# FFN gate weights loaded as 112 partitions on all DMA engines and twice 8 partitions on the lower eight engines

**Chip and metric.** One core of a Trainium2 chip (trn2). The metric is device time in microseconds, the median of several runs; "rounds" are runs of two kernels taken in turn on the same chip. Some executions are slower; only fast runs are compared.

## The reference

One decode step of eight sequences: layer norm, 32 query heads on 8 key/value heads over the last 1,024 positions, output projection, times the silu of a gated FFN. Nearly all of the time is reading 47 MB once (the data queue's packets fill 95.3% of the span on 16 engines): K and V (34 MB), and the weights.

```python
def _A_ref(x, k_cache, v_cache, wq, wo):
    W = min(4096, max(256, Sk // 4))                 # 1024
    q = (x @ wq).reshape(B, Sq, Hq, Dh).transpose(0, 2, 1, 3)
    k = jnp.repeat(k_cache[:, :, Sk - W:, :], rep, axis=1)
    ...
    p = _softmax(scores, axis=-1)
    ...
def _B_ref(x, w_gate, w_up, w_down):
    return (_gelu(x @ w_gate) * (x @ w_up)) @ w_down   # 512 -> 1792 -> 512

xn = _layernorm(x)
return x + _A_ref(xn, ...) * _silu(_B_ref(xn, ...))
```

## The kernel before

All large loads are issued by SyncE on one queue, in the order in which they are needed; the program runs ahead, with eight transfers in flight (the trace has eight completion semaphores, used in turn). The FFN weights come last but for the output weights `wo`.

```python
def load_wide(rows, c0, c1):
    t = wide_slot()                                   # [128, 8192] bf16, one of three buffers
    nc.sync.dma_start(out=t[:, 0 : c1 - c0], in_=rows[:, c0:c1])
    return t

def load_up(w):                                       # 128 rows of 7168 bf16 = 14,336 bytes
    return load_wide(w.rearrange("(p k) n -> p (k n)", k=NDC), 0, NDC * F)
# ... cut ...
for g in range(NGR + 1):                              # NGR = 16 groups of K and V
    if g < NGR:
        v_t[g] = load_kv(A_v_cache, *groups[g])       # 128 rows of 8,192 bytes each
        if g + 2 < NGR:
            k_t[g + 2] = load_kv(A_k_cache, *groups[g + 2])
    if g == NGR - 1:
        wg_t = load_up(B_w_gate)
        wu_t = load_up(B_w_up)
        wd_t = load_down()
    if g == NGR:
        parts = [(0, 16), (16, 24), (24, 28), (28, 30), (30, 31), (31, 32)]
        wo_t = [load_wo(*q) for q in parts[:2]]       # the first takes the gate's buffer
        # ... cut ...
```

The softmax here doesn't subtract the row's maximum and nothing guards it: scores larger than these inputs give would overflow.

## Time and profile before

| | before |
|---|---|
| time, median (range) | 120.83 us (120.68 to 120.94) |
| span of the profiled run | 118.8 us |
| DMA, mean of 16 engines in mid-run | busy all the time, 427 GB/s |
| TensorE, VectorE, ScalarE busy | 73%, 52%, 34% |
| last weight piece lands, engine by engine | 113.90 to 115.50 us |

The lines are in the prediction. The DMA engines never rest (share 1.00 to 1.01 from 20 to 113.5 us), so only their slowest decides. Each transfer is split over engines, and the trace holds one packet record per row and one completion per engine (16 for the gate load of 128 rows, 8 for each of the two loads of `x_sb`, which have 8 rows), without the engine's name. As packets of one engine follow each other without a gap (each starts 3 ns before the recorded end of the last), they can be chained into 16 lanes by their times alone; "lane" below means that. Where packets are lengthened, that overlap scatters up to some 25 ns and two lanes can be swapped, so there a lane is the likeliest chain, and what counts is read from packets and completions without lanes.

Nearly all rows take the same time: of the 4,224 rows of 8,192 bytes on the data queue all but 14 took 309 ns, seven of the 14 longer by 9 ns at most; of the 384 rows of 14,336 bytes all but one took 535 or 540 ns. A "fetch" below is a packet on the queue that the page calls instruction; there are seven in the span, of 16,384 bytes, and the prediction lists when they came and what they cost.

### The profile page before, as it was taken

How to read it: one execution, taken by the hardware profiler on the slowest of the kernel's cores; microseconds unless marked ns; L12 is line 12 of the kernel's file. 1: busy time of each engine (PE TensorE's matmuls, PEld its weight loads, DVE VectorE, ACT ScalarE, POOL GpSimd, SP SyncE). 2: the span in 40 equal slices, each digit the busy share in tenths (PEclk: the TensorE clock that was granted, in tenths of full speed). 3: DMA queues.
4: the chain of work that ended last, by engine and by line, in shares of the span. 5: the costliest groups of instructions: out<-in, count | busy, mean ns of one | idle time of the engine just before them, and what ended most of it. 6: DMA issues, size and time to landing. Idle time of an engine off the chain costs nothing.

```text
span 118.8 us, 2378 instructions
## 1 busy us (share of the span) xinstructions
PE 86.6 (73%) x985; PEld 59.4 (50%) x985; DVE 62.0 (52%) x131; ACT 40.5 (34%) x78; POOL 4.8 (4%) x14
## 2 busy tenths in 40 slices
PE   0005946786989899799799798778959661898680
PEld 0004713653657567577477386456638340334670
DVE  5025645543756856956866764846728336420111
ACT  5000324792442552462462462442524303002000
POOL 5900000000000000000000000000000000000000
PEclk9999999555899999999999999999999996579999
DMA  4999999999999999999999999999999999999950
GB/s 88 437 394 436 419 433 425 422 433 419 428 428 430 422 417 436 417 430 428 419 422 436 425 417 433 428 425 425 422 428 446 419 449 415 440 438 400 409 193 3
DMA packets 6345, 47.61 MB, mean 401 GB/s; under 512 B 816, under 2 KB 1088, under 8 KB 1344
## 3 DMA queue, kind: packets, MB, share of 16 engines
q1 hardware_dynamic: 6304, 47.47, 95.3%
q8 instruction: 7, 0.11, 0.3%
q14 instruction: 2, 0.02, 0.0%
q10 hardware_dynamic: 32, 0.01, 0.0%
HBM read 47.46 MB, written 0.01 MB: 400 GB/s over the span
## 4 chain that ended last, share of the span: by engine, by line
DMA 58%; PE 24%; DVE 7%; ACT 4%; SPq 2%; issue 1%; DVEq 0%
DMA wide_slot<-in_B_w_gate_dram 18%; DMA slot<-in_A_v_cache_dram 16%; DMA slot<-in_A_wo_dram 12%; DMA wide_slot<-in_A_wq_dram 11%; PE t_ps L257 11%; DVE kT L263 4%; PE sc_ps L283 4%; PE o_ps L317 3%; ACT q_all L429 2%; PE a_ps L344 2%; DVE q_all L429 2%; PE big L567 1%; ACT L296 1%; PE sc_ps L273 1%; PE big L445 1%
## 5 line engine op out<-in xcount | busy, mean ns | idle before, releaser
L263 DVE COPY kT<-t_ps 128x1024 bf16<-128x1024 bf16 x48 | 31.7, 688 | 23.3 <-PE t_ps L257 21.4
L257 PE MATMUL t_ps<-ident_f,slot 128*128 128x128 f32 x256 | 38.3, 300 | 2.4 <-DMA slot<-in_A_k_cache_dram 2.2
L257 PEld LDWEIGHTS t_ps<-ident_f,slot 128*128 128x128 f32 x256 | 31.1, 153 | 12.5 <-issue 7.6
L263 ACT COPY kT<-t_ps 128x1024 bf16<-128x1024 bf16 x16 | 16.2, 1012 | 11.6 <-ACT p L296 5.0
L296 ACT ACTIVATE p<-sc_ps 128x512 bf16<-128x512 f32 x16 | 9.6, 597 | 30.1 <-PE sc_ps L283 30.0
L283 PE MATMUL sc_ps<-kT,q_all 128*32 128x512 bf16 x128 | 10.7, 406 | 7.6 <-DVE kT L263 5.8
L304 DVE STREAM_TRANSPOSE pT<-p 128x512 bf16<-128x512 bf16 x16 | 11.2, 703 | 2.7 <-ACT p L296 2.7
L317 PE MATMUL o_ps<-slot,pT 128*32 128x256 bf16 x256 | 9.9, 275 | 1.1 <-DVE pT L304 1.1
L344 PE MATMUL a_ps<-selr,o_sb 128*128 128x16 f32 x64 | 8.4, 263 | 0.0
L283 PEld LDWEIGHTS <-q_all 128*32 128x32 bf16 x128 | 2.0, 95 | 12.4 <-DVE kT L263 8.4
L344 PEld LDWEIGHTS a_ps<-selr,o_sb 128*128 128x128 f32 x64 | 7.8, 192 | 0.0
L225 PE MATMUL t_ps<-ident,xhat 32*128 32x32 bf16 x4 | 0.3, 194 | 10.3 <-DVE xhat L215 10.3
L317 PEld LDWEIGHTS <-pT 128*32 128x32 bf16 x256 | 5.4, 95 | 4.2 <-issue 2.5
L327 ACT COPY o_sb<-o_ps 128x256 f32<-128x256 f32 x16 | 6.0, 377 | 1.3 <-PE o_ps L317 1.3
L273 PE MATMUL sc_ps<-far,hot 4*128 4x512 bf16 x16 | 6.4, 398 | 0.0
L445 PE MATMUL big<-wide_slot,xT 128*32 128x448 bf16 x32 | 2.6, 463 | 4.3 <-DMA wide_slot<-in_B_w_up_dram 3.1
L225 PEld LDWEIGHTS <-xhat 32*128 32x128 bf16 x4 | 0.2, 114 | 10.2 <-DVE xhat L215 10.2
L567 PEld LDWEIGHTS <-og 128*32 128x32 bf16 x128 | 4.1, 97 | 2.2 <-issue 1.1
L366 PE MATMUL t_ps<-q_sb,ident 128*32 128x512 bf16 x14 | 4.8, 497 | 0.0
L353 DVE RECIPROCAL rs<-a_ps 128x32 f32<-128x32 f32 x8 | 2.9, 358 | 3.0 <-PE a_ps L344 3.0
L429 DVE COPY q_all<-t_ps 64x128 bf16<-64x128 bf16 x4 | 2.7, 778 | 2.4 <-ACT q_all L429 1.6
L429 ACT COPY q_all<-t_ps 64x128 bf16<-64x128 bf16 x4 | 2.7, 726 | 2.5 <-DVE q_all L429 2.5
(70 smaller groups left out, 54.2 us busy)
## 6 DMA issues: line engine op xcount, KB each, us to landing
slot<-in_A_k_cache_dram SPq DMA_DIRECT2D x16, 1024.0 KB, 19.6
slot<-in_A_v_cache_dram SPq DMA_DIRECT2D x16, 1024.0 KB, 19.6
wide_slot<-in_A_wq_dram SPq DMA_DIRECT2D x2, 2048.0 KB, 10.6
wide_slot<-in_A_wo_dram SPq DMA_DIRECT2D x1, 2048.0 KB, 12.3
wide_slot<-in_B_w_gate_dram SPq DMA_DIRECT2D x1, 1792.0 KB, 21.4
wide_slot<-in_B_w_up_dram SPq DMA_DIRECT2D x1, 1792.0 KB, 23.2
wide_slot<-in_B_w_down_dram SPq DMA_DIRECT2D x1, 1792.0 KB, 25.0
slot<-in_A_wo_dram SPq DMA_DIRECT2D x1, 1024.0 KB, 14.4
```

Of the source, the lines that this page charges most:

```text
L257: nc.tensor.transpose(kp[:, c * P : (c + 1) * P], kw[:, rp * P : (rp + 1) * P], ident_f)
L263: copy(out=kT_t[g][:, t * 8 * P : (t + 1) * 8 * P], in_=kp.bitcast(BF16))
L273: nc.tensor.matmul(sc, hot.rearrange("n r q -> n (r q)"), far, start=True, stop=False, skip_group_check=True,)
L283: nc.tensor.matmul(sc[32 * t : 32 * t + 32, :], q2_all[:, i, b, e, :, :, :].rearrange("w r n j -> w (r n j)"), kT[:, :, 32 * t : 32 * t + ...
L296: nc.scalar.activation(out=p, in_=sc_t[g], func=ACT.Exp, scale=inv_sqrt_dh, accum_out=acc)
L304: nc.vector.transpose(out=pT, in_=p)
L317: nc.tensor.matmul(o_ps[32 * u : 32 * u + 32, :], pT_t[g][:, m * 32 : (m + 1) * 32], v_t[g][:, m * 256 : (m + 1) * 256], start=(m < 4), st ...
L327: nc.scalar.copy(out=o_sb, in_=o_ps)
L344: nc.tensor.matmul(a_ps[:, 1, m, :], o_t[g + m][:, r * Dh : (r + 1) * Dh], selr[:, r, :], start=(r == 0), stop=(r == 1), skip_group_check= ...
L366: nc.tensor.matmul(idle[0:32, :], ident[:, 0:32], moving[:, 0:512], start=True, stop=True, skip_group_check=True,)
L429: copy(out=q2_all[64 * rr : 64 * rr + 64, i, :, e, rr, :, :].rearrange("p b n j -> p j n b"), in_=qT_ps[64 * rr : 64 * rr + 64, :, e, :, 0 ...
L567: nc.tensor.matmul(acc[a], shifted(og, j, q), wo_t[piece][:, c0 : c0 + DQ], start=(j == rows[0] and q == 0), stop=(j == rows[-1] and q == ...
```

## The change

The seven engines that finish 1.4 us early are to take work from those that finish late. Each of the two loads of `x_sb`, with 8 rows, made 8 packets and 8 completions: it ran on eight engines, here called the lower eight. So 16 of the gate's 128 rows are cut off and sent as two 8-row loads, while 112 rows go to all engines. If the pieces go to the same eight engines as `x_sb` and the 112 rows are dealt out evenly, 7 each, a lower engine has 9 rows and another 7; that was the plan, and the trace names no engine to check it by.

```diff
-    def load_wide(rows, c0, c1):
+    WHOLE, LOWER = [(0, P)], [(0, P - 16), (P - 16, P - 8), (P - 8, P)]
+
+    def load_wide(rows, c0, c1, pieces=WHOLE):
         t = wide_slot()
-        nc.sync.dma_start(out=t[:, 0 : c1 - c0], in_=rows[:, c0:c1])
+        for p0, p1 in pieces:
+            nc.sync.dma_start(out=t[p0:p1, 0 : c1 - c0], in_=rows[p0:p1, c0:c1])
         return t
-    def load_up(w):
-        return load_wide(w.rearrange("(p k) n -> p (k n)", k=NDC), 0, NDC * F)
+    def load_up(w, pieces=WHOLE):
+        return load_wide(w.rearrange("(p k) n -> p (k n)", k=NDC), 0, NDC * F, pieces)
@@
-            wg_t = load_up(B_w_gate)
+            wg_t = load_up(B_w_gate, LOWER)
```

## The prediction

> **What bounds the kernel now.** I read the page's slices first, then its DMA queues, then the chain that ended last, then the waits of the DMA-issuing queue.
>
> The slices and the queue lines:
>
> ```profile
> DMA  4999999999999999999999999999999999999950
> GB/s 88 437 394 436 419 433 425 422 433 419 428 428 430 422 417 436 417 430 428 419 422 436 425 417 433 428 425 425 422 428 446 419 449 415 440 438 400 409 193 3
> q1 hardware_dynamic: 6304, 47.47, 95.3%
> q8 instruction: 7, 0.11, 0.3%
> q14 instruction: 2, 0.02, 0.0%
> ```
>
> The 16 DMA engines are busy from the second slice to the third from the end, at some 427 GB/s, 26.7 GB/s each. TensorE at 73% and VectorE at 52% follow. So the kernel ends when the slowest DMA engine has moved its bytes. The chain of waits, cut to its last pieces, says the same:
>
> ```profile
> 75.69 21.41 DMA wide_slot<-in_B_w_gate_dram
> 97.15 0.94 PE big L445 x16
> ...
> 99.92 14.42 DMA slot<-in_A_wo_dram
> 114.33 0.04 issue
> 114.37 1.56 PE big L567 x32
> 115.96 0.29 DVE tmp L581
> 116.27 0.28 DVE out_sb L582
> ```
>
> After the last weight pieces only 3 us are left. The gate load stands on the chain because line 97 (the large output weight load) takes the gate's buffer, but that issue at 98.13 us comes some 6 us before the engines finish the down weights (103.9 to 105.6), so it starves nothing.
>
> The page gives the mean of the engines; the view by windows shows that they do not finish together:
>
> ```profile
> 110.00:113.50 3.50, 2.48 (x84) 2.36 (x85) 0.49 (x2) 0.00 (x0) 0.00 (x0) 1.00 1.00 401
> 113.50:114.20 0.70, 0.55 (x20) 0.42 (x15) 0.00 (x0) 0.00 (x0) 0.00 (x0) 1.00 0.66 241
> 114.20:115.60 1.40, 1.23 (x30) 1.23 (x30) 0.55 (x2) 0.00 (x0) 0.00 (x0) 1.00 0.32 113
> ```
>
> The DMA share (last column but one) falls from 1.00 to 0.66 to 0.32 before the end. The trace's completion events (one per engine and transfer) say how: of the last weight piece, seven engines complete at 113.90 to 114.13 us, one at 114.59, eight at 115.04 to 115.50. That 1.4 us is what the change is after: hand work from late engines to early ones.
>
> **Who is late, and why.** Ahead of 26 us all 16 engines complete each 1 MB within 0.36 us. Then single engines fall back by about 1.41 us, each just after a 16 KB packet of queue 8 (at 27.2, 42.0, 54.1, 67.0, 81.8, 92.5 and 112.3 us; 0.88 to 0.96 us of transfer, and the row queued beside it takes 0.76 to 1.03 us instead of 0.31 or 0.54); the two packets of queue 14 cost two others 0.5 to 0.85 us. Every other engine advances by exactly 2,453 ns per 1 MB, so the engines can be followed by phase. The two loads of x have 8 rows and put a 512-byte packet on eight engines: those are the "lower eight". Followed to the down weights (108.5 us), lateness in ns is: lower 0, 152, 158, 231, 762, 1199, 1440, 1551; the other eight 94, 169, 215, 225, 1509, 1584, 1606, 1675. The packet at 112.3 makes the 94 late too. So fetches hit both halves: five of nine late ones are upper, four lower.
>
> [...]
>
> **The change part by part.** Bytes are the same. A gate row is 14,336 B; its packet takes 535 ns, and 8 rows 4,260 ns between completions, so 532 ns a row.
>
> (1) Row counts. An upper engine has 7 rows instead of 8: -0.53 us. A lower has 7+1+1=9: +0.53 us. By the phases above: latest upper 1,675-532=1,143 ns; latest lower 1,551+532=2,083 ns. The latest of all goes from 1,675 to 2,083: **+0.41 us**, not a gain, as a lower engine that served a fetch is nearly as late as the latest upper.
>
> (2) Ports. [...] With (1): 2,083+1,800=3,880 ns against 1,675, **+2.2 us**. [...]
>
> (3) 112 rows. [...]
>
> (4) Issues. Two more DMA issues of some 0.33 to 0.43 us on SyncE, which waits anyhow. Completion semaphores go round in eight, so the up and down issues (78.13 and 80.54) each come two places, some 5 us, later; the work then queued is still over 15 us: **0**. The late wo pieces wait for up and down as before.
>
> Sum: +0.4, about +2.2 for (2), 0 to +1 for (3): **+2.7 us, 123.5 us**. All of it reaches the end, as the final pieces need all engines' completions, and TensorE's 1.56 us come after.
>
> **The rivals.**
> - *Balance works:* the unprofiled runs' fetches fall on upper engines and ports don't matter: -0.4 us at best (0.53 per row, less what is exposed), 120.4. For it: the two latest engines are upper. Against it: four lower engines are as late to 0.12 us.
> - *Ports don't bind:* only (1) remains, +0.4 us, 121.2. For it: the trace before shows no port collision. [...] I give these two together 0.3.
> - *Full convoy:* the collisions of (2) at their worst plus (3), +4.6 to 5.5 us, 125.5 to 126.3. [...] Against it: they are 1.5 us out of step. 0.15.
> - *The gate's late arrival becomes the bound:* it lands later by 2 to 4 us, and the large wo load's issue too; there are about 6 us of queued work behind, so only early engines could run dry, and these have slack. It costs nothing unless the gate slips by over 5 us.
>
> **Range and chances.** No change in bytes, so the floor is some -0.4 us; with ports it is +2.2 to +4.6. 2% is 2.42 us, 123.25 us, just under my estimate. Not binding (0.3) and the milder half of the port cases give "same" 0.41; the rest slower 0.57; faster by 2.4 us would need more than all of the 1.4 us at the end, 0.02. Range 121.0 to 125.6.
>
> **What would show it.** Right: 14,336-byte packets of the two 8-row pieces, and rows of the up load beside them on two to four engines, take 1.6 to 2.6 us instead of 0.535; the engines' spread of completions grows from 1.7 to about 4 us just there and stays; GB/s dips in the slices of 91 to 98 us; the gate lands 2 to 4 us later; the last weight piece lands at about 118.2 instead of 115.5. Wrong: all 14,336-byte packets stay at 535 ns, and the last landing moves by 0.4 us or less, or back; then ports do not bind and only row counts do. If packets of the 112-row piece are lengthened, part (3) holds.

The sum came to +2.7 us, 123.5 us: +0.4 for (1) and about +2.2 for (2), which contains the 0.4, and 0.5 out of 0 to +1 for (3). The working of (2) and all of (3) rested on an assumption about which rows collide in SBUF (at a "port", as the text calls it) and how fast they then go. No trace had shown either, so "+1.8 us" (the 1,800 ns left in (2)), the worst case of +4.6 us for (2), 5.5 us with (3), and the 0 to +1 stand without a basis.

## The result

| | before | after |
|---|---|---|
| time, median (range, runs) | 120.81 us (120.68 to 121.22, 6) | 127.16 us (126.81 to 128.22, 6) |
| span of the profiled run | 118.8 us | 125.1 us |
| gate landed on all engines | 97.11 us | 103.37 us |
| last weight piece: mean of the 16 engines' completions | 114.73 us | 119.95 us |
| last weight piece: last completion | 115.50 us | 121.40 us |

The ratio is 1.054 (95% interval 1.049 to 1.059). Ratios here are the mean time of one kernel's fast runs over that of the other's of the same rounds, so not quite the ratio of the medians. The change costs 6.3 us, 5%. It lies outside the predicted range.

The slices of the page after, as in the prediction for before (40 slices, here of 3.1 us):

```profile
DMA  4999999999999999999999999999999999999930
GB/s 100 404 431 440 422 424 430 424 427 424 424 427 430 417 430 422 432 419 427 427 422 424 427 427 432 422 424 427 427 317 243 183 275 431 423 441 405 390 104 3
```

The DMA row looks untouched: 9 throughout. The row below it does not: four slices, from 91 to 103 us, fall to 317, 243, 183 and 275 GB/s. A packet that is held up counts as busy for as long as it lasts, so the DMA share stays at 1 (1.01 from 91 to 103 us, with 242 GB/s moved). The view by windows of before and then of after (us; the last two columns are the DMA share and GB/s):

```profile
91.00:103.00 12.00, 6.63 (x92) 4.20 (x92) 5.55 (x13) 2.44 (x6) 0.00 (x0) 0.83 1.00 428
```

```profile
91.00:98.00 7.00, 5.19 (x59) 3.93 (x58) 2.58 (x8) 1.32 (x4) 0.00 (x0) 0.75 1.08 262
98.00:103.00 5.00, 0.00 (x0) 0.00 (x0) 0.45 (x1) 0.00 (x0) 0.00 (x0) 0.50 0.92 215
...
91.00:103.00 12.00, 5.19 (x59) 3.93 (x58) 3.02 (x9) 1.32 (x4) 0.00 (x0) 0.65 1.01 242
```

At 242 instead of 428 GB/s, 12 x (1 - 242/428) = 5.2 us of transfer are lost there. Outside, the rates are those of before: 427 GB/s from 80 to 91 us and 424 from 103 to 118, against 429 from 80 to 91 and 424 from 103 to 112.

The chain that ended last, after:

```profile
80.64 22.73 DMA wide_slot<-in_B_w_gate_dram
103.37 0.14 issue
103.50 1.69 PE big L450 x16
...
107.01 13.11 DMA slot<-in_A_wo_dram
120.12 0.04 issue
120.16 1.68 PE big L572 x32
```

Its first line is now the second 8-row piece (issued at 80.64), the last of the gate to land, 103.37 - 97.11 = 6.3 us later than before. From there to the end of the span it is 21.7 us in both kernels, so nearly all of the loss lies ahead of 103.4 us. That the two agree to 0.1 us is partly chance: the last weight piece lands only 5.9 us later.

Two terms settle the end. The **mean** completion of the last weight piece moved by 119.95 - 114.73 = 5.22 us, the same as the 5.2 us lost above. The **lateness** of the last engine over the mean went from 0.77 to 1.45 us, +0.68 us. Together 5.90 us, the distance of the two last completions. The rest of the span's 6.3 us lies behind all transfers: from issue to landing the output store takes 1.38 us in both, but from its landing to the last instruction it is 0.84 us before and 1.23 us after. That stretch is 1.23 to 1.29 us in every run with one or two loads more than before, and 1.66 to 1.68 us in those with four more. So it goes with the number of loads; why was not looked into.

And the packets: before, the one long row of 14,336 bytes, beside a fetch, took 1,031 ns, all others 535 or 540. After, 174 rows from 91.4 us on took over 615 ns, up to 1,445, with a middle of 990. They are rows of the 112-row piece, of the 8-row pieces, and of the up load behind them, a plain 128-row load. One lane of after from about 91 us (g a 14,336-byte row, S a completion, durations in ns), a typical one by that chaining:

```
g535 g768 g766 g966 g1011 g984 g1014 S g1012 g1198 g1385 g1013 g882 g665 g535 ...
```

Seven rows of the 112 (up to S), then rows behind it.

### The profile page after: what moved, and what is told of

Its sections match the earlier page's. It is cut to its first block, busy times and chain, and to the rows that moved or that the text cites. A ratio compares the mean times of both kernels' runs of the same rounds, so it can differ in the third digit from the quotient of the medians.

```text
span 125.1 us, 2382 instructions
## 1 busy us (share of the span) xinstructions
PE 87.9 (70%) x985; PEld 59.6 (48%) x985; DVE 61.9 (50%) x131; ACT 40.5 (32%) x78; POOL 4.8 (4%) x14
## 4 chain that ended last, share of the span: by engine, by line
DMA 49%; PE 31%; DVE 9%; ACT 6%; issue 2%; SPq 1%; ACTq 0%; DVEq 0%
DMA wide_slot<-in_B_w_gate_dram 18%; DMA slot<-in_A_v_cache_dram 16%; PE t_ps L262 14%; DMA slot<-in_A_wo_dram 10%; DVE kT L268 5%; DMA x_sb<-in_A_x_dram 4%; PE sc_ps L288 4%; PE o_ps L322 4%; ACT q_all L434 2%; PE a_ps L349 2%; PE big L405 2%; DVE q_all L434 2%; PE big L450 1%; PE big L572 1%; ACT L301 1%
## 5 line engine op out<-in xcount | busy, mean ns | idle before, releaser
L262 PE MATMUL t_ps<-ident_f,slot 128*128 128x128 f32 x256 | 37.6, 295 | 3.5 <-DMA slot<-in_A_k_cache_dram 3.2
L262 PEld LDWEIGHTS t_ps<-ident_f,slot 128*128 128x128 f32 x256 | 29.9, 149 | 13.3 <-issue 6.6
L288 PE MATMUL sc_ps<-kT,q_all 128*32 128x512 bf16 x128 | 10.1, 384 | 7.8 <-DVE kT L268 6.0
L349 PE MATMUL a_ps<-selr,o_sb 128*128 128x16 f32 x64 | 9.2, 277 | 0.0
L450 PE MATMUL big<-wide_slot,xT 128*32 128x448 bf16 x32 | 3.4, 573 | 8.0 <-DMA wide_slot<-in_B_w_gate_dram 6.1
L349 PEld LDWEIGHTS a_ps<-selr,o_sb 128*128 128x128 f32 x64 | 8.6, 210 | 0.0
L450 PEld LDWEIGHTS <-xT 128*32 128x32 bf16 x32 | 1.1, 127 | 9.0 <-issue 9.0
L392 DVE CAST og<-rg_ps 128x256 bf16<-128x256 f32 x1 | 0.7, 727 | 7.1 <-PE rg_ps L385 7.1
```

The lines of the kernel that those rows point to most:

```text
L262: nc.tensor.transpose(kp[:, c * P : (c + 1) * P], kw[:, rp * P : (rp + 1) * P], ident_f)
L288: nc.tensor.matmul(sc[32 * t : 32 * t + 32, :], q2_all[:, i, b, e, :, :, :].rearrange("w r n j -> w (r n j)"), kT[:, :, 32 * t : 32 * t + ...
L349: nc.tensor.matmul(a_ps[:, 1, m, :], o_t[g + m][:, r * Dh : (r + 1) * Dh], selr[:, r, :], start=(r == 0), stop=(r == 1), skip_group_check= ...
L450: nc.tensor.matmul(ps[32 * j : 32 * j + 32, 0:FT], xT[:, k, :], ws[:, k * F + j * FT : k * F + (j + 1) * FT], start=(k == 0), stop=(k == N ...
```

## The experiments

My theory after the result: the rows run at half speed because of where they go, as rows in flight together to certain partitions hold each other up. Rivals: (i) the uneven row counts, (ii) the shape of the loads or the order of their source rows, whatever the destination, (iii) local sharing, in which only the rows that collide slow down, against a collision that holds back all 16 engines.

The texts ahead of the runs say "port theory", and some runs are named for it. A port is an assumption there: a group of partitions whose rows collide. Which partitions make up a group, and which engine writes them, was assumed when the destinations were chosen; no trace shows a port, and the engine numbers are labels too. What the runs can show is which destinations stall and which don't.

Two columns of this table come from the completions of the last weight piece in each profiled run, against before: *stall* is the shift of their mean less what extra bytes cost at 26.7 GB/s per engine; *lateness* is the last engine's distance from the mean (0.77 us before). The stall is good to some 0.1 us: in e9 the lengthened packets add up to about 1.7 us, 0.1 us as a mean of 16 engines, where the column has 0.00.

| run | time, us | before, same rounds | ratio (95%) | extra bytes, us | stall, us | lateness, us |
|---|---|---|---|---|---|---|
| after | 127.16 | 120.81 | 1.054 (1.049-1.059) | 0 | 5.22 | 1.45 |
| e1_112_16 | 126.77 | 120.69 | 1.051 (1.047-1.056) | 0 | 5.71 | 0.87 |
| e2_64_64 | 127.77 | 120.69 | 1.059 (1.057-1.061) | 0 | 5.71 | 1.73 |
| e3_even_odd | 121.43 | 120.69 | 1.007 (1.003-1.011) | 0 | 0.00 | 0.91 |
| e4_extra128 | 123.26 | 120.94 | 1.018 (1.013-1.023) | 2.15 | -0.02 | 0.91 |
| e5_extra112 | 126.62 | 120.94 | 1.046 (1.039-1.052) | 2.15 | 3.06 | 0.92 |
| e6_extra8_near | 125.22 | 120.94 | 1.035 (1.028-1.042) | 0.61 | 2.28 | 1.67 |
| e7_extra8_far | 122.74 | 120.94 | 1.013 (1.008-1.018) | 0.61 | 0.01 | 1.56 |
| e8_extra8_odd (3 fast runs) | 124.88 | 120.69 | 1.036 (1.032-1.040) | 0.61 | 2.29 | 1.39 |
| e9_two_one_port | 122.49 | 120.70 | 1.016 (1.013-1.019) | 0.15 | 0.00 | 1.66 |
| e10_two_own | 122.19 | 120.70 | 1.012 (1.007-1.018) | 0.15 | 0.04 | 0.91 |
| e11_four_one_port | 122.06 | 120.70 | 1.011 (1.009-1.013) | 0.15 | 0.32 | 1.44 |
| e12_four_ports | 123.65 | 120.76 | 1.025 (1.021-1.029) | 0.31 | 1.33 | 1.30 |

All gave the correct result. Runs with "extra" loads are the kernel before, with loads added behind the gate into a ring buffer that nobody reads.

### Is it the uneven row counts?

**e1_112_16**: the changed kernel with the two 8-row pieces joined, so that each engine should have 7 + 1 rows.

```diff
-    WHOLE, LOWER = [(0, P)], [(0, P - 16), (P - 16, P - 8), (P - 8, P)]
+    WHOLE, LOWER = [(0, P)], [(0, P - 16), (P - 16, P)]
```

> The changed kernel with its two 8-row pieces put together: gate as 112 rows and 16 rows, both on all 16 engines (7 rows and 1 row each), so no engine has more rows than another. If the 112-row shape is most of the cost: it loses about 3.3 us in the 112 rows (7 x (1.0 - 0.535)) and 1 to 1.6 us in the 16 rows[...], +4.3 to +5 us (125.2 to 125.8). If the lower eight's row count and the 8-row pieces were the main cost: +3.3 us or less, and near 0 if only uneven rows matter.

126.77 us, 6.1 us over before, and 5.71 us of stall: about all of the loss is there though the rows divide evenly by 16. The lateness is 0.87, near before's 0.77, where after has 1.45: uneven counts are worth some 0.6 us, not 6. My figure of 1 to 1.6 us for the 16 rows was small: rows of that stage took up to 1,656 ns. Rival (i) is out as main cause.

### Is the 112-row piece slow by itself?

**e4_extra128** and **e5_extra112**: 896 KB more as 128 rows, or as 112.

```diff
+            rows = B_w_gate.rearrange("(p k) n -> p (k n)", k=NDC)
+            extra = slot()
+            nc.sync.dma_start(out=extra[:, 0:3584], in_=rows[:, 0:3584])             # e4
+            nc.sync.dma_start(out=extra[0:112, :], in_=rows[0:112, 0:SLOT])          # e5
```

> The kernel before, with one more load behind the gate: 128 rows of 7,168 bytes (896 KB) into an unused buffer. Both theories: 57,344 bytes more for each engine at 26.7 GB/s, so +2.1 us (122.9), every 7,168-byte packet at about 270 ns. It is the yardstick for the 112-row run of the same bytes.

> The same 896 KB as 112 rows of 8,192 bytes into partitions 0 to 111. If the 112-row shape itself is slow (each row at about twice its time, as the trace after shows for 14,336-byte rows), 7 rows cost 7 x 0.6 instead of 7 x 0.31 us: +2.1 us for the bytes and about +2 us for the shape, +4.1 in all (124.9). If the 112-row piece is slow in the changed kernel only because the 8-row pieces behind it block it, +2.1 us as in the yardstick.

In its transfers e4 costs its bytes and nothing else (stall -0.02 us). e5 costs 3.4 us more than e4, of which 3.06 us are stall: the 112-row shape is slow with no 8-row piece near. The windows of e4 and then of e5:

```profile
95.00:97.00 2.00, 1.06 (x10) 1.05 (x10) 0.84 (x3) 0.30 (x1) 0.00 (x0) 0.72 0.96 405
97.00:99.00 2.00, 1.80 (x17) 0.61 (x16) 0.16 (x1) 0.07 (x1) 0.00 (x0) 0.50 1.12 477
```

```profile
95.00:97.00 2.00, 1.14 (x10) 1.13 (x11) 0.76 (x3) 0.37 (x1) 0.00 (x0) 1.00 1.07 304
97.00:99.00 2.00, 0.00 (x0) 0.00 (x0) 0.24 (x1) 0.00 (x0) 0.00 (x0) 0.50 1.00 201
```

The dip is to half (201 GB/s, from 426 between 91 and 95 us), and it lasts into the up load: 60 rows of 14,336 bytes were lengthened too, 14 of them the gate's last and 46 of the up load. I had expected about 2 us for the shape; it was 3.1 us, since the rows beside and behind it pay as well.

### Is it the destination, or the shape and the source?

**e6_extra8_near**, **e7_extra8_far**, **e8_extra8_odd**: four more 8-row loads. Source rows, sizes and count are the same in all three; only the destination partitions differ.

```diff
+            extra = slot()
+            for i in range(4):                               # e6: 96 to 127, neighbours
+                r = slice(96 + 8 * i, 104 + 8 * i)
+                nc.sync.dma_start(out=extra[r, :], in_=rows[r, 0:SLOT])
# e7: for i, q in enumerate((0, 1, 2, 3)):      out=extra[q : q + 32 : 4, :]   (0 to 31, four apart)
# e8: for i, q in enumerate((64, 65, 66, 67)):  out=extra[q : q + 32 : 4, :]   (64 to 95, four apart)
```

> The kernel before with four more loads of 8 rows x 8,192 bytes behind the gate, each into 8 neighbouring partitions (96-103, 104-111, 112-119, 120-127), lower eight engines only. By bytes alone a lower engine has 4 x 0.31 = 1.24 us more; the latest lower goes from 1.55 to 2.79 us of lateness, against 1.675 for the latest of all now: +1.1 us (121.9). Port theory[...]: rows take 2.3 to 2.6 times as long as in the changed kernel, another +1.5 to +2 us, so +2.6 to +3.1 (123.4 to 123.9). Rival (destination does not matter): the same as the run with far partitions.

> The same four loads, same source rows, same engines, but each into 8 partitions four apart (0,4,..28; then 1,5,..29; 2..; 3..)[...]. Port theory: no collision, packets at 309 ns, +1.1 us (121.9), clearly below the near run. Rival, that any 8-row load on half the engines is slow by its shape or its source rows: the same time as the near run.

> As the far run (four extra loads of 8 rows of 8,192 bytes[...]), but into partitions 64 to 95[...]. Port theory: [...]the lower engines' rows take 2 x 0.31 us and they lose 4 x 0.62 = 2.5 us instead of 1.24: +2.3 us by the lateness of before (1.55 + 2.5 - 1.675), between the far run (122.7) and the near run (125.2). If only eight neighbouring partitions are harmful: as the far run.

The windows of e6, of e7 and of e8, in this order:

```profile
95.00:97.00 2.00, 1.03 (x10) 1.02 (x10) 0.87 (x3) 0.29 (x1) 0.00 (x0) 1.00 1.17 283
97.00:99.00 2.00, 0.03 (x4) 0.03 (x7) 0.12 (x1) 0.00 (x0) 0.00 (x0) 0.96 0.92 216
```

```profile
95.00:97.00 2.00, 1.10 (x10) 1.10 (x10) 0.79 (x3) 0.37 (x1) 0.00 (x0) 0.97 1.05 443
97.00:99.00 2.00, 1.74 (x17) 0.59 (x16) 0.20 (x1) 0.01 (x1) 0.00 (x0) 0.50 0.96 412
```

```profile
95.00:97.00 2.00, 1.01 (x10) 1.01 (x10) 0.88 (x3) 0.28 (x1) 0.00 (x0) 1.00 1.12 297
97.00:99.00 2.00, 0.18 (x4) 0.14 (x7) 0.12 (x1) 0.00 (x0) 0.00 (x0) 0.89 1.05 249
```

The same source rows into neighbouring partitions cut the rate of the whole core to half (216 GB/s from 97 to 99 us); into partitions 0 to 31, four apart (412 GB/s there), no packet is lengthened there but one at a fetch (the extra rows take 309 ns each) and the stall is 0.01 us. Rival (ii) falls for the 8-row loads: the destination decides. e7's profiled span is 2.25 us longer: 0.62 us of mean for its bytes, 0.79 us of lateness for uneven counts, and 0.84 us after the output has landed, where all runs with four more loads lose it. The timed +1.8 us, with +1.1 expected, is a little less.

e8 is the finer test: its rows are as far apart as e7's, but go to partitions 64 to 95. It stalls like e6 (2.29 and 2.28 us) and takes about as long. I had it between e7 and e6; it was at e6. So it isn't only neighbouring partitions that hurt, and spacing alone doesn't help: which partitions the rows go to decides. Why these and not those was not shown, as no record names the engine or the destination of a row.

**e2_64_64** and **e3_even_odd**: the gate in two loads of 64 rows, once as halves and once as even and odd partitions.

```diff
-    WHOLE, LOWER = [(0, P)], [(0, P - 16), (P - 16, P - 8), (P - 8, P)]
+    WHOLE, LOWER = [(0, P)], [(0, P // 2), (P // 2, P)]                          # e2
+    WHOLE, LOWER = [(0, 1)], [(0, 2), (1, 2)]   # (first, step); t[p0:P:st, ...] # e3
```

> The gate as partitions 0-63 and then 64-127, each on all 16 engines with 4 rows each. Port theory: [...]every row takes 2 x 0.535 = 1.07 us: 8 rows lose up to 8 x 0.535 = 4.3 us, somewhat less where early engines are already in the second half, +3 to +4.3 us (123.9 to 125.1). Rival (only shapes that do not divide evenly over the ports are slow): 0.

> The gate as the even partitions and then the odd ones, again 4 rows to an engine[...]. If the number of ports reached by the load decides: 0 to +0.5 us. If what decides is which ports are written at the same moment[...]: row times near 1.07 us again and +2 to +4.3 us. [...]

Of e2 and then of e3:

```profile
95.00:97.00 2.00, 0.77 (x16) 0.52 (x16) 0.00 (x0) 0.00 (x0) 0.00 (x0) 0.68 0.99 229
...
99.00:101.00 2.00, 0.52 (x3) 0.41 (x2) 0.99 (x3) 0.00 (x0) 0.00 (x0) 0.50 1.03 229
```

```profile
95.00:97.00 2.00, 1.04 (x10) 0.94 (x9) 0.85 (x3) 0.30 (x1) 0.00 (x0) 1.00 1.06 452
```

Both have 64 rows a load, 14,336 bytes a row. As halves the core runs at 229 GB/s, about half of e3's 452 in the same window; its lengthened rows took about 1,035 ns, for 535. As even and odd partitions not one packet beside that at a fetch was lengthened, and the stall is 0.00. My range for e2 (+3 to +4.3 us) was too low; it was +7.1: early engines already in the up load were slowed until the last late one had sent its last gate row, at about 102.8 us. e3's +0.7 us is hardly in a transfer: in its profiled run, 0.57 us longer, the last weight piece lands 0.13 us later and 0.43 us come after the output has landed.

### Who pays: the rows that collide, or everyone?

In e6, lanes that had only rows of ordinary 128-row loads were slowed like the others. But it has eight extra rows a load, going to 32 partitions in all, so each of these lanes may have collided with an extra row itself. The next four runs have only two or four extra rows a load.

```diff
+            extra = slot()                    # e9: four loads of 2 rows, into 0-3 and 32-35
+            for i, q in enumerate((0, 2, 32, 34)):
+                r = slice(96 + 2 * i, 98 + 2 * i)
+                nc.sync.dma_start(out=extra[q : q + 2, :], in_=rows[r, 0:SLOT])
# e10: q in (0, 1, 2, 3): out=extra[q : q + 8 : 4, :]                        2 rows a load, four apart
# e11: q in (0, 32): 4 rows a load, out=extra[q : q + 4, :]                  neighbours
# e12: i in range(4): 4 rows a load, out=extra[64 + i : 80 + i : 4, :]       64 to 79, four apart
```

> The kernel before with four extra loads of 2 rows of 8,192 bytes behind the gate, on engines 0 and 1 only, into partitions 0-1, 2-3, 32-33, 34-35[...]. Theory A, a collision slows only the engines that write the crowded port: engines 0 and 1 need 0.62 us a row, 2.5 us in all, every other row stays at 535 ns; the end moves by at most the lateness of two engines, +0 to +2 us depending on which they are. Theory B, a crowded port holds back all 16 engines[...]: up rows of nearly all engines go to about 1.07 us for some 2.5 us, and the summed rate falls to half of 427 GB/s there; the kernel loses about 1.2 us on all engines and the two engines' rows on top, +1.2 to +2.5 us. The count of lengthened packets decides, not the time.

> Control[...]: the same four loads of 2 rows on the same two engines, but into partitions 0 and 4, 1 and 5, 2 and 6, 3 and 7[...]. Both theories: no lengthened packet beside those at instruction fetches; the two engines have 1.24 us more, +0 to +1.4 us at the end depending on how late they are.

> Two extra loads of 4 rows of 8,192 bytes, engines 0 to 3, into partitions 0-3 and 32-35[...]: the same 64 KB into the same partitions as with two engines. Theory A (local): engines 0 to 3 need up to 1.24 us a row, others nothing. Theory B (all held back, at the pace of the most crowded port): rows of all engines go to 1.5 to 2.1 us while four engines share the port, for about as long as the port needs for 8 rows (2.5 us): a deeper and shorter dip than with two engines, loss 1.2 to 2 us on all engines.

> The kernel before with four extra loads of 4 rows of 8,192 bytes behind the gate, engines 0 to 3, into partitions 64, 68, 72, 76 (then 65.., 66.., 67..)[...]. Local sharing only[...]: rows of eight engines at about 0.62 us (8,192 bytes) or 1.07 us (14,336 bytes), the eight bystanders at 535 ns throughout. Spill that grows with the number of crowded ports: the bystanders' rows too, well over the 10 to 20% seen with one port and four engines[...]. At the end +1 to +2.5 us in either case.

The windows of e9 and then of e12:

```profile
95.00:97.00 2.00, 2.00 (x17) 1.75 (x9) 0.00 (x0) 0.37 (x1) 0.00 (x0) 0.50 0.99 413
97.00:99.00 2.00, 2.00 (x19) 0.91 (x19) 0.99 (x3) 0.00 (x0) 0.00 (x0) 0.50 1.00 416
```

```profile
95.00:97.00 2.00, 1.06 (x10) 1.05 (x10) 0.83 (x3) 0.32 (x1) 0.00 (x0) 1.00 1.22 333
97.00:99.00 2.00, 0.49 (x8) 0.32 (x11) 0.16 (x1) 0.00 (x0) 0.00 (x0) 0.92 0.86 263
```

Lanes from the packet records by that chaining (k an 8,192-byte row, 309 ns where nothing holds it up; g and S as above; the first lane of each pair carries extra rows, the second has none):

```
e9   S k309 S k309 S k494 S k602 S g821 g542 g535        e9   g535 g535 S g535 g535 g535 g535
e11  S k309 S k673 S g1235 g542 g535                     e11  g535 S g609 g633 g535 g535
e12  S k309 S k309 S k559 S k643 S g958                  e12  S g535 g881 g1104 g859 g609
```

With two extra rows at a time into neighbouring partitions (e9), two lanes slow down and the other fourteen stay at 535 ns: local. With four at a time into neighbours (e11), the other lanes rise to about 600 to 655 ns for one or two rows. With four at a time into partitions four apart (e12), the packets in flight at 96.8 us settle it without any lane: four extra rows of 626 to 641 ns, and on the other twelve engines a row of 1,041 to 1,119 ns each. If each extra row collided with one other row, as local sharing would have it, four of the twelve could be slow and eight would be bystanders at 535 ns; all twelve are slow. The same count in e9 at 97.0 us finds two slow rows (602 and 847 ns) and fourteen of 535 ns. From e9 (stall 0.00 us) to e11 (0.32) to e12 (1.33) more of the other rows wait, and for longer. The control e10, two at a time into partitions four apart below 8, shows no lengthened packet but the one at a fetch, and only some 0.1 us more lateness. Its timed +1.5 us, as much as e11's +1.4, is larger than its transfers account for: the last weight piece lands 0.3 us later. In the profiled run another 0.84 us come after the output has landed, which leaves some 0.3 us of the timed difference open.

## Why the prediction was wrong

**Right.** The bound; the sign; that balance was not to be had; that the two extra issues hold up no transfer (427 GB/s from 80 to 91 us and 424 from 103 to 118, as before). Step (1), row counts, said +0.41 us: lateness moved by +0.68, and by +0.58 between e1 and after. That rows to certain destinations hold each other up was right, and so in kind were the marks named for it: a dip, lengthened packets of the up load, a spread of completions that stays. Their sizes were not: the dip lasted to 103 us and not 98, the spread of the last piece grew from 1.6 to 2.9 us and not to 4, and the gate landed 6.3 us later and not 2 to 4. That passed the 5 us beyond which the fourth rival saw the gate's lateness as a bound, yet it cost nothing more: the next large load was issued at 105.23 us, ahead of the first engine's end of the down weights (108.72), and the rate held at 424 GB/s.

**Wrong: step (3) in size.** It put 0 to 1 us on the 112-row piece. Alone (e5, rows of 8,192 bytes) it stalls 3.06 us; for rows of 14,336 bytes that scales to 3.06 x 14,336 / 8,192 = 5.4 us, an estimate, and as much as the whole stall of the changed kernel. In the changed kernel its rows took about 1,000 ns each on every lane. My working had the rows queue up neatly, an assumption that no run had shown, and so found little loss. What e8 and e2 show is rows at about half rate (extra rows some 580 to 630 ns for 309 in e8, gate rows 1,035 for 535 in e2).

**Wrong: the locality in step (2).** Its working charged the collision to the lower engines and four others, and gave early ones slack. e12 shows twelve other engines at half rate (1,041 to 1,119 ns for 535) with four extra rows in flight. So the stall is not a delay of some engines, part of which the 1.4 us of slack at the end could swallow; it moves the mean of all sixteen. That is why the mean completion moved by 5.22 us. A single row was even held up less than predicted (at 98.7 us, with 8-row pieces in flight, all sixteen rows take 1.12 to 1.37 us, and no row ever over 1.45, where I said 1.6 to 2.6), but all rows of all engines paid for 11 us.

**Small: step (4).** It said 0; the 0.4 us after the output store came with the two extra loads.

**Slips in the working.** In the sum, "+0.4, about +2.2 for (2)" counts the 0.4 twice, as the 2.2 contains it; the total of +2.7 is right with 0.5 for (3). "Four lower engines are as late to 0.12 us": by its own list one is (1,551 against 1,675 ns), the next is 0.24 us off.

**The rivals.** "Full convoy" (+4.6 to +5.5 us, given 0.15) came nearest, though it put nearly all of the convoy on the 8-row pieces. "Ports don't bind" and "balance works" are refuted by e7 against e6.

**Left open.** Which rows an engine takes of a load, and which partitions it writes, is in no record; that the 112-row piece is slow because of where its rows go is argued from e2, e3, e6, e7 and e8, not seen. How the 5.22 us divide between the 112-row piece and the 8-row pieces is not separable either, as late engines are still in the first when early ones are in the second; e1 only shows that a 16-row piece in place of the two 8-row ones is no better. By time, not by cause: the mean engine ends its seven rows of the 112 at 99.41 us, 3.7 us later than before's gate less one row (96.21 - 0.53), and picks up some 1.5 us after that. What makes the other engines wait was not found: e9, e11 and e12 give its doses, not its place.

**Could the intent work?** No version beat the kernel before. e7 shows how to give eight engines more work at almost no stall (0.01 us): 8-row loads into partitions 0 to 31, four apart. But the gate's rows must land in all 128 partitions, and the same loads cost 2.29 us of stall into 64 to 95 (e8), and 2.28 us into 96 to 127 as neighbours (e6). That is argued from e6, e7 and e8; no kernel tried it on the gate itself.

## What to carry to other kernels

When DMA is at its limit, look at GB/s and at packet durations, not at the DMA busy share: it stood at 0.92 to 1.08 in the kernel after while the rate was 215 to 262 GB/s instead of 428. Splitting a 128-partition load by partition ranges is not neutral: here halves cost 7.1 us (e2) and even and odd partitions 0.7 us (e3), for the same bytes and rows a load. Before cutting a load to move rows between engines, measure the destination on its own, with extra loads into a buffer that nobody reads: four 8-row loads stalled 0.01 us into one set of partitions and 2.29 us into another (e7, e8), and four rows at a time into partitions 64 to 79, four apart, slowed the rows of all sixteen engines (e12).
